# Draining attention's output by head halves, with new order strings for the five engines

## The chip, the cores and the metric

One NeuronCore of a Trainium2 chip runs the whole program. The metric is the device time of one execution in microseconds (us); the kernel before is given by three executions and their median.

## The reference, cut to what matters

The inputs are q, k, v of shape (4 batches, 8 heads, 768 tokens, 64), eight memory keys and values per head, and the weights of two layers of width 512.

```python
for c in range(24):                                  # chunks of 32 queries
    k_ctx = k[:, :, l_start:r_end]                   # 16 keys to the left, 8 to the right
    scores = scale * q_c @ concat([mem_k, k_ctx]).T  # 64 keys a query
    a = softmax(scores)
    out[:, :, c_start:c_end] = a @ concat([mem_v, v_ctx])
x = out, heads side by side                          # (4, 768, 512)
gate = sigmoid(sum_k conv_w[k] * x shifted by k)     # causal convolution, 5 taps
x = (gate * (x @ w_val)) @ w_out
xn = (x - mean) / sqrt(var + 1e-6) * g_ln
out = x + relu(xn @ w_ch1) @ w_ch2                   # 512 -> 2048 -> 512
```

## The kernel before, in words

The 3072 tokens are 24 sub-blocks of 128 tokens (n = 0 to 23). A block (j = 0 to 12) is one sub-block at both ends and two in between. Each sub-block goes through attention (`attend`, or `attention32` in float32 for the first ones), each block then through mixing (`mix_steps`: convolution, gate, two projections, layer norm) and the feed-forward part (`ffn`: `ch1` and then `second`, or from j = 3 on `products` and `fast_finish`, a scheme of seven products instead of eight). Matmuls are split: a float32 value is held as two float16 parts, and three of the four part products are summed.

**What attention leaves.** The last matmuls of a sub-block (L541, in float32 L445) write two PSUM tiles `pv[0]` and `pv[1]`, one for each group g of 64 tokens; partitions 0 to 63 hold one head of a pair (e = 0) and 64 to 127 the other (e = 1). `activations` copies them with a scale into `xT` in four instructions of 64 partitions x 256 values. ScalarE (ACT) does all four at L395 for n under 2 (`EVAC_ACT`) and n of 8 and up (`NEVAC`); for n = 2 to 7 VectorE (DVE) does those with e = 1 at L397. All of them done, ACT and DVE make the float16 parts `x` (L547, L548).

**PSUM banks.** `bank` hands out banks in rotation. From j = 3 on (`fast[0]`) only the two buffers of the tag "ps" rotate, so `pv[0]` and `pv[1]` take both, and whoever calls `bank` next gets the buffer of `pv[0]`, the one after it that of `pv[1]`. For n = 9, 11, ... 21 the next two in program order are the scores of the next sub-block (`s_ps`, L349) and a second projection of mixing (`yps`, L619).

**What sets the order.** Every instruction gets a one-letter label while the program is made (`mark`): a and b attention of even and odd sub-blocks, x and y mixing of even and odd blocks, f the first layer of the feed-forward part with its evacuation, g its second layer and end, t sums of weights, m, p, q the conversion of the mixing weights, of w_ch1 and of w_ch2, l and w loads, s the start. `pin` then reads one string for each engine (`ORDER`): "b48f24a48" means the next 48 instructions with label b, then 24 with f, then 48 with a; "a+2" takes the one that stands two places further on among those left of its label. Each instruction gets a dependency on the one before it in the string, so the string is the engine's order. An engine works in that order; one that waits holds up all behind it.

**Names of the steps below.** In the start: convolution taps L583, gate tanh L587, gate product L603, projection `yps` L619 with its copy L624, layer norm L626 to L646, transposed result `xnT` L651, weight conversion L230 and L231. Later: `ch1` matmuls `c_ps` L804, their copy `ft` L717, operand parts `hb`/`w` L721 to L728, `products` matmuls `acc` L769, transposing DMAs of the probabilities `pT` (L521) and of the normed rows `xn` (L666).

Of the kernel before, what the change touches and what calls it, by code (L numbers as in the profile page):

```python
# [49 lines left out]
PLAN = "w1 a4 l1 a1 w3 m2 w1 m1 a1 x1 w1 1_1 m1 l1 x1 w1 x1 w1 x2 w1 x3 a2 w1 x1 1_1 a1 m1 a2 w1 a1 x1 1_1 a3 1_2 x1 1_3 2_1 x2 1_1 l1 x4 f2 w1 1_1 m1 x1 w2 1_1 2_1 m1 1_1 2_2 x1 2_1 x1 1_1 2_1 f1 a1 w1 m1 a1 2_2 f1 x1 f2 2_1 w1 a2 1_1 2_1 l1 f1 a4 m1 w1 x1 f1 2_3 w1 a2 1_2 x1 1_1 2_4 f1 a1 x1 f2 x1 f2 a2 f1 x1 a2 x1 a1 f2 x1 a1 x3 a1 f1 a1 x1 a1 f1 a1 x1 f1 a1 x1 f1 a1 f3 a1 f1 a2"  # L50
ORDER = {
    "PE": (
        "s24a+16a+16a+16a+16a+16a+16a+16a+16a+16a+16a+16s8a69a+4a+4a+4a+4a+4a+4a+4a+4a+20a+20a+20a+20a+20a+20a+20a+20a+20a+20a+20"
        "a+20a+20a+20a+20a+20a20m16m+16x6m8x8b16x2m8x4b4a16b16x4mp24f3f+13f+13f+13a4p8f3a16p16f2y3p8f14q8f6p8y8fy2q8y3py3q16y2q8"
        "y3b17f5q8f11gf14g3q8gf2gq8gb4gqag3a16b16g5ff+23a4f23a10ba6g12f71g2g+1g+1gx10b48x14f12x12f12g6f14x12f10x6gag12x18b48f12g6"
        "f24a48f12g54a48bf48y24f12g12f12b48g6f36g6f24y24g12af48b48y24a48g12f12g30a48g12bg6x36f60x12f36b48f12g10f24g8f12g24ag12f12"
        "b48f24a48x24f12g84a48g18bg12f96b48y24g10f12g8f36y24ag54b48g12f12a48y24f36g18bg36a48g30b48x12f48x12f24x12f24g10x12f48g20a"
        "f12b48g24a48f12x24f24g30bg42a48g42f12b48f36y24f24g18f24y24f48g12ag12f12b48f24a48y24f12g72bg30a48g24b48f36x12f12x12f36x12"
        "f12x12g30f24g12f24b48af24g18f12a48x24g12f12g12bg30a48g54f96b48y36g10y12f48g20ag24f24b48g18a48y24f24g12bg84a48f60b48f36"
        "x36f12g42f12x12f24ag18b48f36a48x24f12g66bg18a48g24f72g18f12g12f12b48g12f24y48f24g30b48f12y24f36g24x12g42x24g30x12f96g30"  # L60
        "f24g12f12g12x6g6f36x6f24g78f36g30f156g96"),
    "DVE": (
        "s2a7s2a2m2bm+2m+2mxx+3xx+2xx+1x3x+3xx+2xmx2bxabx2pbmbm+2bm2bpxmxbx3ax6ax3paxa3papm3pb+3ma2pyy+3yy+2yy+1qypy2y+3ypyy+1y2p"
        "yqpqympyp3q2mpmqy2pybb+2ybpyqba+3x+20ybypy3by3pybybyqybpqmqpyqbq2pq2aa+2a3qyaqaba2qbaqbgfb3qbx+22a2b2xtxtbtxfx2txbax+2ft"
        "xx+1x2t+2fx2bxbqtb+6xbxy+20bt2xb2txtxtbtxbtat+1a2qftat2xafx2axa2xbxa+8xbx3axax5a3xa2txty+22fabtt+2xtft3gt2ga2t2t+1yab3t"
        "b2y2fby4b2fy2t3bftby+3ytyty+1yfybyt2t+1t3b2ybt2t+1fbya3bfa2t2yt2yb2t2a2yaa+7a2y2a4y2t+2x+20ty2ay3fy6tyt3fbyx+22tayxtxbx"
        "b2xtb2g2b2xt+1xtx3x+3xx+2f5bfb+7bxbf3x2f2bxb3fbxx+1a3faf2xafa3a+7fxa2fax2a3x8ax6f3y+20f2xy+22fxb4y2bg4g+1x+20g2by+2byy+1"
        "b2faf4b+8fy3bfyf4ybyfy2b2y3b2a2bayby+1ya2fafaf2yfaa+8a2fa2y2a3by8ay6fbx+22bf4yb6fyag4b+7b2xg+1g2b2xx+2xf4x+1x2fbfx2bx+3x"
        "f2y+20bf2xx+1fx3fxx+1a2fa2xa4a+7axf2af2axa2fx5ax5ax5b3y+22b3xf5b2xfbb+7g4g+1yg2yay+2yy+1ybyf2bf2y2y+3b2fybfyy+1y2byf3bf2"
        "yfy+1a2x+20yafa2fa2faya+7f2a3fa2y2ay2ay12bfyf2x+22bfb2fb3yfb2b+8gbg2agx2g+1g2x+2xx+1x2bf5x6fb3x2bxby+20f3xfbf2x+1x2a3f5"  # L70
        "a5a+8a2bfa4x2ax2ax12b2fxf4b3xfb2g3y+22gg+1g2y2y+2abf2b+7f3yy+1b2fby4f2y+3f2x+20y2fy+1y3fb4a3ya2y+1yf5a3a+7x+22ya2fy2a4"
        "y14af3yf2b2fyb6g4g+1g2xbb+7f3xfb2afx+2xy+20fb2x+1xbx3x+3f4bx2x+1xfbx2fxx+1a5xfa3f2a+7xa2f2a4xfx7ax8f3xbf2b2xb3fbg3y+22g"
        "g+1g2y2y+2yy+1yf3yf3x+20b2b+8b2y2y+3ybabyy+1b2y2byfbyf5y+1yfyf4bxfyx2x+1x2x+2xy2x+1y14f3x2x+1xf2xyfxg2xg2g+1g2xf4x2f8xf4"
        "x2fx10fx3f6gf2g2fgg+1gfg5"),
    "Activation": (
        "s3a2msm2a4x4mbpaxbpxpb2ap3b2pa2b+1y2qypybmm+1q2yfq2mpyqpmyfpq2pba+1pab+3yp2f2pqb+3yqabqbq2b2fqa2bx2bx2qfbt+1af2b+2btfax2"
        "a2xbqt+1taxafaxb2a+2axfbfabxt+1tb2at+1a2yty3bfb2b+2f2bft+1ta2yfayt+1btfyab2a2fya+2bt+1ya2b3tfya5yt+1xtb2x3bb+2f+1f4af2b"
        "a2fxbf+1f2x2a3a+2b4faxbf+1xfab2fx2bfx2a4y2gy2b2abf+1fb+2f2af4bf+1a2ybyf2aya2a+2b5faybyab2f+1f2y2b3yfaya4xgb+2bax3f+1f6ab"
        "afxf+1f2xa3a+2b2xb3afx2b3af+1f2x4b2fbb+2a4gy2ay2f+1f2a2baf4byfyf+1f2aya2a+2b4faybyaf+1fbfby2by2b2fba3b+2a2gx2f+1f2a3x2b"
        "f4bxfxf+1xf2a3b2a+2fb6ax2af+1f2x3a2xfb3a2gyay2b+2f+1fyf2bf3a2fyaf+1bf2ya3ya+2b4fb3yabyaf+1f2y3fyb2gbb+2a4xf+1f2a2xbafx2"  # L80
        "f2afbfxf+1fxfa3a+2xb6axfaxbf+1fbfx4fb2abb+2ga3y3f+1f6ayb2y2ff+1f2yb5x2fxyxyf+1fyfy3fgf+1x2f7f+1f2x2ff+1x2f3gf4"),
    "Pool": (
        "as4s+2s2ab2ta+1ab2gbaba+1ab2aba+1ba2b3a"),
    "SP": (
        "s+1s3w2l2w2l3w2lw2lw2lqwlw3q2l2waqlyaa+1yay2b+2ga2b+2b+2b2a+2a+2a+2x2axaxg2b+2b+2b3a+2a+2a+2a2y4g2b+2b+2b+2b2a+2a+2a+2a2"
        "x4b+2b+2b+2g2b2a+2a+2a+2a2y4b+2b+2b+2bgba+2ga+2a+2a2x4b+2b+2b+2b2a+2a+2g2a+2a2y4g2b+2b+2b+2b2a+2a+2a+2a2x4b+2gb+2gb+2b2"
        "a+2a+2a+2ay2ay2g2b+2b+2b+2b2a2x4gb2gy4g2x2g4"),
}
PASSES = ((0, 0), (0, 1), (1, 0))

# [19 lines left out]
def chunk_attention_moe_kernel(ctx: ExitStack, tc: tile.TileContext,  # L110
# [276 lines left out]

    def activations(n, xT, pv, c_pv):
        c0 = KW - 1
        for g, t in enumerate(pv):  # L390
            for e in range(2):
                pp = slice(e * 64, (e + 1) * 64)
                o = xT[pp, :, c0 + g * 64:c0 + (g + 1) * 64].rearrange("p a (c q) -> p a c q", q=CHUNK)
                if e == 0 or n < EVAC_ACT or n >= NEVAC:
                    nc.scalar.activation(out=o, in_=t[pp, :, :, e, :], func=AF.Copy, scale=c_pv if isinstance(c_pv, float) else c_pv[pp])  # L395
                else:
                    nc.vector.tensor_scalar(out=o, in0=t[pp, :, :, e, :], scalar1=c_pv if isinstance(c_pv, float) else c_pv[pp], scalar2=None,  # L397
                                            op0=ALU.mult)


    def attention32(n, d, u):
# [46 lines left out]
        if n == 0:  # L448
            fill(FILLS[3])
        activations(n, xT, pv, 1.0)  # L450
        if not d["f32"]:
            xs = xT[:, :, KW - 1:KW - 1 + SUB]
# [13 lines left out]
    def attend(n, d, u):  # L466
# [625 lines left out]
```

## Time and profile before

| what | us |
|---|---|
| three executions, median (lowest to highest) | 725.04 (724.04 to 728.56) |
| the profiled execution, its time | 727.59 |
| the profiled execution, span from its first to its last instruction | 725.5 |
| TensorE matmuls busy (share of the span) | 705.8 (97%) |
| VectorE, ScalarE, GpSimd busy | 621.6, 462.1, 15.5 |

The times of rows are those of the profiled execution, counted from its first instruction. PE is TensorE's matmuls, PEld its weight loads, DVE VectorE, ACT ScalarE, POOL GpSimd, SP the engine that issues most DMAs. L395 is line 395 of the kernel before. A granted clock of 1.00 is 2.4 GHz and one of 0.50 is 1.2 GHz. Matmuls overlap in the records, so the mean duration of one is longer than the distance from one to the next.

### The profile page before, as it was taken

The numbers are of one execution on the slowest core, as the hardware profiler recorded it, in microseconds if no ns is written. First come the engines' busy times: TensorE is split into PE (matmuls) and PEld (weight loads), VectorE is DVE, ScalarE is ACT, GpSimd is POOL, SyncE is SP. The second block draws the span as 40 slices with busy tenths as digits, with TensorE's granted clock in tenths as the row PEclk, the third lists the DMA queues.
The fourth block names the chain that finished last, engine by engine and source line by source line (L and its number), as shares of the span: only waits on it lengthen the run. The fifth ranks groups of instructions, "written<-read, shape, count | busy, mean of one in ns | idle before, by whom it ended". The sixth has DMA issues, their size and how long they took to land.

```text
span 725.5 us, 18122 instructions
## 1 busy us (share of the span) xinstructions
PE 705.8 (97%) x7629; PEld 570.4 (79%) x7629; DVE 621.6 (86%) x1339; ACT 462.1 (64%) x734; POOL 15.5 (2%) x37
## 2 busy tenths in 40 slices
PE   8899999999999999999999999999999999999998
PEld 7687768657758888878778878878878878878897
DVE  4889999999999979989979989879988987885443
ACT  4578775656665885884776786775787685562330
POOL 2010010000000000000000000000000000000000
PEclk9999999999999999999999999999999999999999
DMA  9997323241242323232322233133033012101001
GB/s 348 414 410 289 93 44 109 55 119 42 44 96 81 98 58 95 55 63 74 111 38 74 49 100 102 18 93 111 16 93 112 17 30 31 31 19 42 2 15 44
DMA packets 64448, 67.76 MB, mean 93 GB/s; under 512 B 47856, under 2 KB 48112, under 8 KB 64368
## 3 DMA queue, kind: packets, MB, share of 16 engines
q1 hardware_dynamic: 64080, 66.59, 30.8%
q8 instruction: 59, 0.97, 0.6%
q14 instruction: 21, 0.17, 0.1%
q10 hardware_dynamic: 288, 0.02, 0.0%
HBM read 49.30 MB, written 6.29 MB: 77 GB/s over the span
## 4 chain that ended last, share of the span: by engine, by line
PE 43%; DVE 32%; ACT 9%; DMA 4%; issue 3%; DVEq 0%; ACTq 0%
PE c_ps L804 18%; PE acc L769 12%; DVE gt L583 5%; PE val L601 4%; PE yps L619 4%; PE acc L849 3%; DMA xn<-xh 3%; DVE w L293 2%; ACT xT L395 2%; ACT bd L499 1%; PE s_ps L349 1%; DVE vs L526 1%; DVE bd L500 1%; DVE bs L626 1%; DVE ks L503 1%
## 5 line engine op out<-in xcount | busy, mean ns | idle before, releaser
L804 PE MATMUL c_ps<-xn,w 128*128 128x256 f16 (+1 forms) x2304 | 255.3, 268 | 3.1 <-DMA xn<-xh 2.5
L804 PEld LDWEIGHTS <-w 128*128 128x128 f16 x2304 | 216.0, 98 | 32.8 <-DMA xn<-xh 3.4
L583 DVE SCALAR_TENSOR_TENSOR gt<-xT,cw_sb,gt 128x256 f32<-128x256 f32 (+1 forms) x208 | 87.5, 457 | 0.9
L769 PEld LDWEIGHTS <-hb 128*128 128x128 f16 x756 | 73.0, 98 | 11.5
L769 PEld LDWEIGHTS <-w 128*128 128x128 f16 x756 | 72.8, 98 | 11.8 <-ACT w L727 2.3
L717 ACT ACTIVATE ft<-c_ps 128x512 f32<-128x512 f32 x72 | 40.8, 592 | 48.3 <-DVE y L787 16.5
L849 PE MATMUL acc<-w,hb 128*128 128x512 f16 (+2 forms) x280 | 64.3, 374 | 0.7 <-DVE hb L818 0.7
L769 PE MATMUL acc<-w,hb 128*128 128x256 f16 (+1 forms) x360 | 64.6, 278 | 0.0
L601 PE MATMUL val<-x,wv 128*128 128x256 f16 (+1 forms) x528 | 60.0, 268 | 0.9 <-DVE x L548 0.9
L769 PE MATMUL acc<-w 128*128 128x256 f16 x342 | 58.8, 273 | 0.0
L619 PE MATMUL yps<-wo,hg 128*128 128x512 f16 x252 | 56.7, 379 | 0.1
L601 PEld LDWEIGHTS <-wv 128*128 128x128 f16 x528 | 49.6, 98 | 7.2 <-issue 1.1
L769 PE MATMUL acc<-spare,hb 128*128 128x256 f16 (+1 forms) x324 | 54.9, 276 | 0.0
L769 PE MATMUL acc<-spare,w 128*128 128x256 f16 x324 | 53.7, 273 | 0.0
L619 PEld LDWEIGHTS <-hg 128*128 128x128 f16 x252 | 24.0, 98 | 27.7 <-DVE hg L607 0.6
L849 PEld LDWEIGHTS <-hb 128*128 128x128 f16 x264 | 25.2, 98 | 19.7 <-DVE hb L818 1.5
L727 ACT ACTIVATE hb<-ft 128x1024 f16<-128x1024 f32 x18 | 18.9, 1052 | 26.7 <-DVE ft L726 26.6
L395 ACT ACTIVATE xT<-pv,c_pv 64x256 f32<-64x256 f32 x70 | 32.4, 465 | 4.9 <-PE pv L541 4.0
L727 ACT ACTIVATE w<-ft 128x1024 f16<-128x1024 f32 x18 | 19.0, 1054 | 22.5 <-DVE ft L726 22.4
L362 ACT ACTIVATE sc<-sc,c_exp 128x512 f32<-128x512 f32 x19 | 13.7, 719 | 29.3 <-DVE sc L361 22.3
L500 DVE SCALAR_TENSOR_TENSOR bd<-qt,s,bd 64x512 f16<-64x512 f32 x38 | 28.3, 745 | 3.1 <-ACT bd L499 2.3
L499 ACT ACTIVATE bd<-qt,s 64x512 f16<-64x512 f32 x38 | 27.1, 713 | 1.9 <-DVE s L200 1.5
(188 smaller groups left out, 1209.8 us busy)
## 6 DMA issues: line engine op xcount, KB each, us to landing
vt<-in_v_dram SPq DMA_DIRECT2D x24, 512.0 KB, 4.9
kt<-in_k_dram SPq DMA_DIRECT2D x24, 384.0 KB, 3.8
qt<-in_q_dram SPq DMA_DIRECT2D x24, 256.0 KB, 2.8
out_dram<-y SPq DMA_DIRECT2D x23, 256.0 KB, 2.3
w<-in_w_ch_dram SPq DMA_DIRECT2D x5, 1023.5 KB, 9.3
spare<-in_w_ch_dram SPq DMA_DIRECT2D x4, 1023.8 KB, 13.0
w<-in_w_ch_dram SPq DMA_DIRECT2D x4, 1023.8 KB, 14.1
spare<-in_w_ch_dram SPq DMA_DIRECT2D x3, 1023.5 KB, 7.7
```

The costliest lines, as they stand in the source:

```text
L293: nc.vector.scalar_tensor_tensor(out=lo, in0=w, scalar=s, in1=hi, op0=ALU.mult, op1=ALU.subtract)
L395: nc.scalar.activation(out=o, in_=t[pp, :, :, e, :], func=AF.Copy, scale=c_pv if isinstance(c_pv, float) else c_pv[pp])
L499: nc.scalar.activation(out=hi, in_=src, func=AF.Copy, scale=s[pp, 0:1])
L500: nc.vector.scalar_tensor_tensor(out=lo, in0=src, scalar=s[pp, 0:1], in1=hi, op0=ALU.mult, op1=ALU.subtract)
L583: nc.vector.scalar_tensor_tensor(out=o, in0=xT[:, hp, 0:n, kk:kk + SUB], scalar=cw_sb[:, kk, hp:hp + 1], in1=o, op0=ALU.mult, op1=ALU.add)
L601: nc.tensor.matmul(out=t[:, u, 0:T], lhsT=l, rhs=r, start=(x == 0), stop=(x == len(todo) - 1))
L619: nc.tensor.matmul(out=t, lhsT=l, rhs=r, start=(x == 0), stop=(x == len(todo) - 1))
L717: nc.scalar.activation(out=ft[:, at:at + 2, :].rearrange("p x (m n) -> p m x n", m=2), in_=t.rearrange("p (m x n) -> p m x n", m=2, x=2), ...
L727: nc.scalar.activation(out=o[0][1], in_=ft, func=AF.Copy)
L769: nc.tensor.matmul(out=o, lhsT=l, rhs=r, start=first, stop=(p == half // 2 - 1 and u2 == 1 and end[t] == x))
L804: nc.tensor.matmul(out=t[:, u * T:(u + 1) * T], lhsT=l, rhs=r, start=(x == 0), stop=(x == len(todo) - 1))
L849: nc.tensor.matmul(out=a[:, 0:n], lhsT=l, rhs=r, start=(first and x == 0), stop=(end and x == len(todo) - 1))
```

## The change

The loops of `activations` change places: first both groups' halves with e = 0, then both groups' halves with e = 1. The strings of all five engines are replaced; each holds the same number of every label as before, in another order. Nothing else changes. The core of the diff, with TensorE's strings whole and the first line of VectorE's and ScalarE's:

```diff
     "PE": (
-        "s24a+16a+16a+16a+16a+16a+16a+16a+16a+16a+16a+16s8a69a+4a+4a+4a+4a+4a+4a+4a+4a+20a+20a+20a+20a+20a+20a+20a+20a+20a+20a+20"
-        "a+20a+20a+20a+20a+20a20m16m+16x6m8x8b16x2m8x4b4a16b16x4mp24f3f+13f+13f+13a4p8f3a16p16f2y3p8f14q8f6p8y8fy2q8y3py3q16y2q8"
-        "y3b17f5q8f11gf14g3q8gf2gq8gb4gqag3a16b16g5ff+23a4f23a10ba6g12f71g2g+1g+1gx10b48x14f12x12f12g6f14x12f10x6gag12x18b48f12g6"
-        "f24a48f12g54a48bf48y24f12g12f12b48g6f36g6f24y24g12af48b48y24a48g12f12g30a48g12bg6x36f60x12f36b48f12g10f24g8f12g24ag12f12"
-        "b48f24a48x24f12g84a48g18bg12f96b48y24g10f12g8f36y24ag54b48g12f12a48y24f36g18bg36a48g30b48x12f48x12f24x12f24g10x12f48g20a"
-        "f12b48g24a48f12x24f24g30bg42a48g42f12b48f36y24f24g18f24y24f48g12ag12f12b48f24a48y24f12g72bg30a48g24b48f36x12f12x12f36x12"
-        "f12x12g30f24g12f24b48af24g18f12a48x24g12f12g12bg30a48g54f96b48y36g10y12f48g20ag24f24b48g18a48y24f24g12bg84a48f60b48f36"
-        "x36f12g42f12x12f24ag18b48f36a48x24f12g66bg18a48g24f72g18f12g12f12b48g12f24y48f24g30b48f12y24f36g24x12g42x24g30x12f96g30"
-        "f24g12f12g12x6g6f36x6f24g78f36g30f156g96"),
+        "s32a+16a+16a+16a+16a+16a+16a+16a+16a+16a+16a+16a69a+4a+4a+4a+4a+4a+4a+4a+4a+20a+20a+20a+20a+20a+20a+20a+20a+20a+20a+20"
+        "a+20a+20a+20a+20a+20a20m16m+16m8x14b16x6m8a12p8a4b14p8mb6x4p8f3f+13f+13f+13a4p8f3a16p24f22p8y16pq8yq8ygyfy5q8b17f5q16f11"
+        "q8f6gq8g2f2q8f6g2b4qaf2a16b16g10ff+23a4f23a10ba6g12f47g2b48f36g+1g+1x48f26g8x6af10g6f12x18f24b48g12a48g4f12g44a48bg6f48"
+        "y24g12f12b48f12g12f36y12f12y12f12g6f12g6af24b48y24a48g12f24g24a48g24bx24f84x24f12b48f48g30af36b48f12g12a48x24g84a48g12b"
+        "g30f84b48f12y24g30f36y12f12ag24y12g6f12b48g24a48y24f36bg54a48g30b48x24f48x12f48x12g18f48g24ag30b48f24a48x24f24g30a48g42b"
+        "g24f60b48f24y12f12y36f48g30af12g12f12b48g12f12a48y24f12g48bg66a48f72g10b48f24g20x24f12x12f36x12ag12f12b48g12f12a48x24f24"
+        "g60ba48g54f96b48g10y12g8y12f12g12f36y24ag24f12b48f24a48y24g6f12g42bg12a48g54f84b48g10f12x24f36x12f12g20x12ag24f12g6b48"
+        "f12g12a48x24f24g72a48g24bf96b48g42f48g12y48f24b48g6f12y24f12g78x48g30f84g18f12g12f48x6g12x6g12f36g6f12g108f84g12f84g36"
+        "f24g48"),
     "DVE": (
-        "s2a7s2a2m2bm+2m+2mxx+3xx+2xx+1x3x+3xx+2xmx2bxabx2pbmbm+2bm2bpxmxbx3ax6ax3paxa3papm3pb+3ma2pyy+3yy+2yy+1qypy2y+3ypyy+1y2p"
+        "sa5sa2s2a2m2bm+2m+2mxx+3xx+2xx+1x3x+3xx+2x4mxbxbpbmab2m+2xbxpxaxm2xbx3ax3mxaxaxapxap2am3p2a2b+3yy+3yy+2yy+1ypmyqyy+3ypy"
...
     "Activation": (
-        "s3a2msm2a4x4mbpaxbpxpb2ap3b2pa2b+1y2qypybmm+1q2yfq2mpyqpmyfpq2pba+1pab+3yp2f2pqb+3yqabqbq2b2fqa2bx2bx2qfbt+1af2b+2btfax2"
+        "s4a2m3a4x4mbpxbaxp3ab3p2bpa2y2pqfb+1y2mq2m+1qyqpmbpyq2ypa+1fbqpmpfypapqb+3b+3b2fqaypq3b2fqbab2axqfxfxt+1xa2b+2abftx2faqx"
...
     def activations(n, xT, pv, c_pv):
         c0 = KW - 1
-        for g, t in enumerate(pv):
-            for e in range(2):
+        for e in range(2):
+            for g, t in enumerate(pv):
                 pp = slice(e * 64, (e + 1) * 64)
                 o = xT[pp, :, c0 + g * 64:c0 + (g + 1) * 64].rearrange("p a (c q) -> p a c q", q=CHUNK)
                 if e == 0 or n < EVAC_ACT or n >= NEVAC:
```

## Rows read from the trace of the kernel before

**Rows 1.** The page: engines' busy time, and TensorE's costliest group

```profile
PE 705.8 (97%) x7629; PEld 570.4 (79%) x7629; DVE 621.6 (86%) x1339; ACT 462.1 (64%) x734; POOL 15.5 (2%) x37
...
L804 PE MATMUL c_ps<-xn,w 128*128 128x256 f16 (+1 forms) x2304 | 255.3, 268 | 3.1 <-DMA xn<-xh 2.5
```

**Rows 2.** Busy time by stage: stretch, PE, PEld, DVE, ACT, POOL, clock, DMA

```profile
0.00:50.00 50.00, 42.48 (x494) 37.15 (x494) 36.16 (x88) 27.25 (x39) 7.30 (x15) 0.93 0.98 389
50.00:225.00 175.00, 172.81 (x1590) 121.12 (x1589) 171.60 (x364) 118.13 (x183) 3.38 (x10) 1.00 0.37 109
225.00:700.00 475.00, 468.60 (x5274) 391.80 (x5273) 405.52 (x874) 313.96 (x508) 4.82 (x14) 1.00 0.24 60
700.00:725.50 25.50, 21.96 (x278) 20.36 (x275) 8.31 (x15) 2.77 (x5) 0.00 (x0) 1.00 0.09 32
```

**Rows 3.** TensorE's waits, 225 to 700 us: us in total, times, longest

```profile
PE c_ps L804 <- DMA xn<-xh: 2.3, 3, 0.9
PE acc L769 <- ACT w L727: 1.7, 2, 1.0
PE val L601 <- DVE x L548: 0.9, 1, 0.9
PE c_ps L804 <- ACT ft L717: 0.6, 1, 0.6
PE s_ps L349 <- ACT xT L395: 0.3, 1, 0.3
PE acc L769 <- DVE w L728: 0.2, 1, 0.2
```

**Rows 4.** Timeline of the start: start, duration, instruction, idle before it

```profile
18.76 3.49 DVE L583 SCALAR_TENSOR_TENSOR gt<-xT,cw_sb,gt 128x128 f32<-128x128 f32 x13
...
22.18 1.22 DVE L231 SCALAR_TENSOR_TENSOR wo<-w,spare 128x1024 int32<-128x1024 int32 x1
...
24.81 0.63 ACT L587 ACTIVATE gt<-gt 128x512 f32<-128x512 f32 x1 [0.28 <-DVE gt L583]
...
25.87 0.74 DVE L603 SCALAR_TENSOR_TENSOR gt<-gt,val 128x256 f32<-128x256 f32 x2
...
26.43 5.37 PE L619 MATMUL yps<-wo,gt 128*128 128x512 f32 x8 [2.30 <-DVE gt L603]
...
32.46 0.69 DVE L626 BATCH_NORM_STATS2 bs<-y 128x6 f32<-128x512 f32 x1 [1.75 <-ACT y L624]
...
36.98 0.55 DVE L646 TENSOR_SCALAR xh<-y,mv,rt 128x512 f32<-128x512 f32 x1
...
37.67 2.05 PE L651 MATMUL xnT<-eye,xh 128*128 128x128 f32 x8 [1.61 <-DVE xh L646]
```

**Rows 5.** Stretches of the start at a lower clock, columns as in rows 2

```profile
26.40:32.50 6.10, 6.07 (x16) 3.07 (x16) 4.35 (x12) 2.24 (x4) 0.00 (x0) 0.72 1.00 414
...
37.60:42.50 4.90, 4.83 (x42) 4.79 (x43) 4.33 (x7) 2.45 (x2) 0.00 (x0) 0.68 1.00 396
```

**Rows 6.** Timeline of one handover of banks, after sub-block 19

```profile
524.50 0.85 PE L541 MATMUL pv<-pT,vs 64*128 64x64 f16 x46 [0.17 <-DMA pT<-p]
...
525.35 1.15 ACT L525 ACTIVATE vs<-vt,s 128x1024 f16<-128x1024 f32 x1 [1.57 <-PE pv L541]
...
526.41 1.91 ACT L395 ACTIVATE xT<-pv,c_pv 64x256 f32<-64x256 f32 x4
...
527.39 0.95 PE L349 MATMUL s_ps<-ks,bd 128*64 128x64 f16 x48
...
528.37 1.89 PE L619 MATMUL yps<-wo,hg 128*128 128x512 f16 x8
```

**Rows 7.** Timeline of two of the waits of rows 3

```profile
379.23 0.28 PE L769 MATMUL acc<-wo,w 128*128 128x256 f16 x1 [0.77 <-ACT w L727]
...
389.40 1.80 PE L601 MATMUL val<-x,wv 128*128 128x256 f16 x15 [0.90 <-DVE x L548]
```

More of the change, by code (lines that the diff above doesn't have):

```diff
@@ L61 @@
-        "f24g12f12g12x6g6f36x6f24g78f36g30f156g96"),
-    "DVE": (
-        "s2a7s2a2m2bm+2m+2mxx+3xx+2xx+1x3x+3xx+2xmx2bxabx2pbmbm+2bm2bpxmxbx3ax6ax3paxa3papm3pb+3ma2pyy+3yy+2yy+1qypy2y+3ypyy+1y2p"
[L64 to L74, printed above, removed]
@@ L75 @@
-    "Activation": (
-        "s3a2msm2a4x4mbpaxbpxpb2ap3b2pa2b+1y2qypybmm+1q2yfq2mpyqpmyfpq2pba+1pab+3yp2f2pqb+3yqabqbq2b2fqa2bx2bx2qfbt+1af2b+2btfax2"
[L77 to L81, printed above, removed]
+        "s32a+16a+16a+16a+16a+16a+16a+16a+16a+16a+16a+16a69a+4a+4a+4a+4a+4a+4a+4a+4a+20a+20a+20a+20a+20a+20a+20a+20a+20a+20a+20"
@@ new lines @@
+        "g24f60b48f24y12f12y36f48g30af12g12f12b48g12f12a48y24f12g48bg66a48f72g10b48f24g20x24f12x12f36x12ag12f12b48g12f12a48x24f24"
+        "g60ba48g54f96b48g10y12g8y12f12g12f36y24ag24f12b48f24a48y24g6f12g42bg12a48g54f84b48g10f12x24f36x12f12g20x12ag24f12g6b48"
+        "f12g12a48x24f24g72a48g24bf96b48g42f48g12y48f24b48g6f12y24f12g78x48g30f84g18f12g12f48x6g12x6g12f36g6f12g108f84g12f84g36"
+        "f24g48"),
+    "DVE": (
+        "sa5sa2s2a2m2bm+2m+2mxx+3xx+2xx+1x3x+3xx+2x4mxbxbpbmab2m+2xbxpxaxm2xbx3ax3mxaxaxapxap2am3p2a2b+3yy+3yy+2yy+1ypmyqyy+3ypy"
+        "y+1qy3pqpypmpyp2q2pm2ypyqyqybb+2yb3y2py2byqby3pa+3y3pybqbqpqabq2ma+2a3q2ybpqax+20x+22ayaqpaqbgaqbfb3qb4a2ty+20xtxbxtfx2t"
+        "xfx+2xx+1bax2bx2tt+2xtxfxqb+6xtxbfbxtbtabta2ta2bxa3btxtfqx2t+1xtxtxy+22xb2x3a+8xax2ax3ataxaba2ftxatxtt+2tft3ba2b2tbytagy"
+        "tytt+1by2tgyfb3t2ytybfytbtftx+20y+3ybyy+1bt2t+1fyby2t3fbtybty2ba2t+1t2ataya2b2a2ta+7tfayay3ayta2yayt+2y2ayty6tyf2t3ybt2y"
+        "tx+22ax6b4t+1xgx2x+3gtb2xx+2x2f2bf3bxfb+7b2xf5b4fbxa3f2x+1a2f2axa2a+7fxa6fx15axy+20y+22f4xbfxfby2b3g4g+1bg2b3f5y+2yay+1"
+        "y2fb+8bybx+20yf5yb3fb2y4a2yayfbf2yy+1fa5y2a+8a2fba3fyay4ay5ay2by4bfbf3bfbyb3fyag4g+1g2b+7b2x+22xb2xx+2xx+1f2xy+20f3xb2f"
+        "x2x+3x2f5x+1bx2fx2x+1a3xa2f3xa2faa+7fa2faxba2xax2ax12f2xf4xb7y+22g4g+1g2bb+7afy2b2y+2fybf2b2fy+1y2fybyy+3yx+20f3yf2y+1y3"
+        "fyby+1a2fa3f3yax+22ayfaa+7a2fa4by13ay3fyf2b3f2b3yfb2g4g+1g2x2x+2b+8fxf4ax+1b2fxb5fx2f2bxfx4fx3fxx+1a3fa2xa2faa+8faxaf2a3"
+        "xaxafx2ax6y+20x7f4y+22b4fb2xfb2g4g+1g2bb+7f5y2y+2x+20afyy+1y4y+3b2fybyb3fy+1f3y3fbyy+1a3f2ayafa3fa+7ya2bax+22afayafy3a"
+        "y12b3ybf5ybfb2g4g+1g2bb+7xf2af3xx+2xy+20bx+1bfx3bfxfx+3bfbfbfx2x+1xfx2bxx+1a3fa2f2a2x2faa+7fa2fabaxa2x6ax9y+22f3xf3xbgb2"
+        "g3g+1g2b4ybf2ab+8f2yfy+2yy+1fby3bfyfy+3y2y+1b3yb2f2yf2ybyy+1yf3yfx+20f2by2xy2x2x+1xy2fy6xy4f2yf2x+2yxfg4g+1g2x+1x2x+1x4"
+        "f6x2f2x2f6xfx4f3xf3xf2x8fg4g+1fgfg2f2g3"),
@@ new lines @@
+    "Activation": (
+        "s4a2m3a4x4mbpxbaxp3ab3p2bpa2y2pqfb+1y2mq2m+1qyqpmbpyq2ypa+1fbqpmpfypapqb+3b+3b2fqaypq3b2fqbab2axqfxfxt+1xa2b+2abftx2faqx"
+        "a2fat+1bx2tb2a+2b2axf2abxt+1bta2yay2t+1tfb3f2b+2ybt+1tfa3fyby2t+1ta2f2b2aa+2bt+1y2a2bftyba4yxt+1abtx3b3b+2f+1f6bxa2fab"
+        "f+1f2a2xaxa+2b5fa2x2f+1f2b2x2bx2fa4y3gb2abb+2f+1f3af3bayaff+1bf2aya2y2a+2b7afy2baf+1f2yb2yfby2a5xga2xb+2bf+1f2afxbxf4f+1"
+        "x2f2xa3a+2b5fax2ab2f+1f2x3afxb3gbb+2a4f+1fyfy2bfyf3a3bfyf+1f2y2a3a+2b4fab3y2f+1f2aby3byfb2ga2b+2a2x2f+1xf2a2fabfxf2abfx"
+        "f+1f2xa3a+2b5xb2axfbxaf+1f2x4afba3bgby4b+2af+1f6ba3bfyf+1f2y2a3a+2b7ayfyabf+1f2y2b2y2fa3bga2x2b+2f+1f3bx2f3a2bfaf+1fxfa3"
+        "x2b2a+2b3faf+1x2af2x3fxb3agbab2a2f+1yf2b+2ay2f4yb2ff+1f2y3b4fx2bf+1y2xf2xy4fgf+1f4xf2x2ff+1f2xff+1f3x2gf4"),
@@ L82 @@
     "Pool": (
-        "as4s+2s2ab2ta+1ab2gbaba+1ab2aba+1ba2b3a"),
+        "s4s+2s2a2b2a+1batbab2ga+1ab3aa+1abab2ab"),
     "SP": (
-        "s+1s3w2l2w2l3w2lw2lw2lqwlw3q2l2waqlyaa+1yay2b+2ga2b+2b+2b2a+2a+2a+2x2axaxg2b+2b+2b3a+2a+2a+2a2y4g2b+2b+2b+2b2a+2a+2a+2a2"
-        "x4b+2b+2b+2g2b2a+2a+2a+2a2y4b+2b+2b+2bgba+2ga+2a+2a2x4b+2b+2b+2b2a+2a+2g2a+2a2y4g2b+2b+2b+2b2a+2a+2a+2a2x4b+2gb+2gb+2b2"
-        "a+2a+2a+2ay2ay2g2b+2b+2b+2b2a2x4gb2gy4g2x2g4"),
+        "s+1s3w2l2w2lwl2w4lw2lqw3l2q2wlal2qyaa+1a2y3b+2gab+2a+2b+2b2x2a+2a+2a2x2b+2b+2b2g2ba+2a+2a+2a2y4b+2b+2b+2b2a+2a+2ga+2ga2"
@@ L88 @@
+        "x4b+2b+2b+2b2g2a+2a+2a+2a2y4b+2b+2b+2bgba+2ga+2a+2a2x4g2b+2b+2b+2b2a+2a+2a+2a2y4b+2b+2b+2b2g2a+2a+2a+2a2x4b+2b+2b+2bg2b"
+        "a+2a+2a+2a2y4b+2gb+2b+2b2ga2x4g2b2y4g2x2g4"),
 }
```

## The prediction

> **What bounds the kernel now.** I read the page's first part, then busy time by stage, then who TensorE waits for, then the timeline at those places. The page shows PE busy for 705.8 of 725.5 us [rows 1]. By stage, PE is idle for 50 - 42.48 = 7.5 us in the first 50 us, for 175 - 172.81 = 2.2 from 50 to 225, for 475 - 468.60 = 6.4 from 225 to 700 and for 25.5 - 21.96 = 3.5 at the end, where the last result is scaled and sent [rows 2]. So TensorE sets the end everywhere after the start, with VectorE close beside it from 50 to 225 (171.60 of 175), and a reordering of the same instructions can only change 19.6 us of idle time and what a lower clock costs. The clock was not at its upper level in two stretches of the start: the mean grant was 0.72 over 6.1 us and 0.68 over 4.9 us, each behind a wait [rows 5]. Had the upper level held, they would have been 6.1 x 0.28 + 4.9 x 0.32 = 3.3 us shorter at most.
>
> The sum is made against the profiled execution: 727.59 us, that is its span of 725.5 and 2.1 around it. It lies 2.55 above the median of the runs shown, 725.04; I carry the difference over to the median.
>
> **The edit of the loops.** It adds and removes no instruction. For n = 2 to 7 it doesn't do what it says: ACT has the e = 0 halves and DVE the e = 1 halves, each in group order before and after, so no engine's order changes. For the other 18 sub-blocks ACT's four copies run 0/0, 1/0, 0/1, 1/1 (group/half) in place of 0/0, 0/1, 1/0, 1/1. The bank of `pv[0]` is then free after the third copy, not the second; that of `pv[1]` after the fourth, as before. Four copies took 1.91 us, 0.48 each [rows 6], so the first bank is handed over 0.48 us later.
>
> This matters where the next user of the bank comes at once: after sub-blocks 9, 11, ... 21, seven places, of which rows 6 show one. There `pv` ended at 525.35, the copies began at 526.41 (ACT first did the 1.15 us of L525), the second was done at 526.41 + 0.96 = 527.37 and `s_ps` began at 527.39: it took the bank the moment it was free. The fourth was done at 528.32 and `yps` began at 528.37 [rows 6]. In the new string TensorE has exactly 24 matmuls of 256 columns between `pv` and `s_ps` at each of the seven places ("b48f24a48", "b48g12f12a48" and the like; before it was 18 to 54). One takes 255.3 / 2304 = 0.111 us [rows 1], so they last 2.66. The third copy is done (start of the copies after `pv`'s end) + 1.43 later. With the 1.06 of rows 6 that is 2.49: no wait. The copies began 1.39, 1.07, 2.03, 1.07, 3.11, 1.06 and 2.86 us behind `pv` at the seven places; with the same lateness the new order waits 0.2 + 0 + 0.8 + 0 + 1.9 + 0 + 1.6 = 4.5 us. That is the upper end; the lower is nothing, if ACT's new string starts them in time. It moves what delayed the copies: a `hb` of 1.04 us that stood among them at the fifth place goes behind, and so does the 1.15 us of L525, into their middle, at the seventh. I take 0.6, near the lower end, as at the place shown.
>
> Here a rule of the Trainium skill speaks against the edit. What the rows show: the bank of `pv[0]` was written again 0.02 us after its second copy ended [rows 6]. "Perfetto Trace Analysis", section Optimizing Tensor Performance, says that independent matmul groups should rotate through different PSUM banks so that the copying of one overlaps the matmuls of the next. Draining both banks side by side holds both longer, so by the rule the edit loses up to the 4.5 us above; by the place shown it loses nothing. It is the slower rival below.
>
> **The strings in the start.** Before, the chain that ends PE's 2.30 us wait is: taps L583 (13 from 18.76, three more behind a conversion and a maximum), tanh L587 at 24.81, gate product L603 at 25.87, `yps` at 26.43 [rows 4]. The new DVE string runs all 16 taps together ("x4mxbxb" in place of "xmx2bxabx2"): 13 took 22.18 - 18.76 = 3.42, so 16 take 4.21 and end at 22.97; the conversion of 1.22 comes next, the tanh of 0.63 runs beside it, and the first product starts at about 24.2, 1.7 us sooner. PE's second eight gram matmuls (0.6 us) move behind `yps`, so its wait shrinks from 2.3 to about 1.2. What is late next is the layer norm: from L626 at 32.46 to the end of L646 at 37.53 it took 5.07 us, for which PE waited 1.61 [rows 4]. The new string puts a conversion (1.22), two softmax passes of 0.7 and some small ones inside that chain, about 2.8 more, and moves 16 gram matmuls (1.4 us of PE) ahead of `xnT`. Net: 1.7 sooner, 2.8 later, 1.4 of work done meanwhile, some 0.3 gained; with a shorter first wait a part of the 3.3 us of lower clock may come back. Bounds: from 1.5 lost (the 2.8 in full against 1.3 of cover) to 0.3 + 3.3 = 3.6 gained. I take 1.0 gained, near the lower gain, since a second wait stays.
>
> **The strings from 50 us on.** From 225 to 700 TensorE waited nine times for over 0.15 us by the groups shown, 6.0 us in all, mean 0.67 [rows 3]. Where the new string puts the waiting matmul later or its producer sooner, a wait goes. The `acc` at 379.23 waited 0.77 for L727 [rows 7]; L727 now stands ahead of two copies of 0.7, which covers it. The `val` at 389.40 waited 0.90 for L548 [rows 7]; `val` now comes 36 matmuls later, 3.9 us. Read so place by place, the waits for `val`, for L727 (one whole, the other by half), for `s_ps` after L395, for L728 and one of three for the transposed `xn` go: 0.9 + 1.3 + 0.3 + 0.2 + 0.7 = 3.4.
>
> What comes in their place can't be read from the rows of before. The strings also bring matmuls forward past work that their producers still have ahead, by 1 to 6 us in some 20 places; many of these producers only waited, and come forward too. From below it costs nothing; from above each of 20 places costs the mean wait, 13.4. DVE (86% busy) and ACT (64%) [rows 1] have room to follow, so I take a fifth: four waits of 0.67, 2.7 us. In the last stage nothing changes: TensorE's last 24 matmuls, their scaling and the output transfer stay.
>
> **Sum.** -1.0 (start) - 3.4 (waits gone) + 0.6 (banks) + 2.7 (new waits) = -1.1. The profiled execution would go from 727.6 to 726.5, the median from 725.04 to 723.9.
>
> **Rivals.**
> *A clear gain.* The new strings take away nearly all they can: four fifths of 6.4 + 2.2, 6.9 us, and 3.0 in the start with the clock: 725.0 - 9.9 = 715.1. For it: all seven handovers now have the same cover, and the start's first wait is shortened. Against it: the same producers at the same durations, and DVE already busy for 98% of the stretch from 50 to 225 [rows 2].
> *Slower: the banks come late.* Place: `s_ps` behind `pv`, seven times. Price: the 4.5 us above; and where a late `s_ps` makes the softmax and its transposing DMA late, the next `pv`, which waited for such a DMA for 0.17 us at 524.50 already [rows 6], pays it once more, 9.0 in all. It decides once the copies begin over 1.2 us behind `pv`'s end. 725.0 + 4.5 = 729.5, or 734.0 carried on. Against it: only 0.3 us of waits for L395 were seen [rows 3]. The rule of the Trainium skill quoted above is the reason to take it seriously.
> *Nothing.* The strings' gains and new waits cancel: 725.0, between 723 and 727.
>
> **Chances.** Forecast 0.55, its own range 720.5 to 728; clear gain 0.15; banks late 0.18, half of it carried on; nothing 0.12. A measurement of this kernel can tell about 1%, 7.25 us. Faster than 717.8 are most of the clear gain and a sliver of the forecast, 0.14; slower than 732.3 is the carried half of the bank case, with a sliver of the forecast, 0.11; the rest, 0.75, is the same within 1%. Range: 716.5 to 732, which cuts off about a tenth on either side.
>
> **What would show it.** Right: PE busy for 704 to 707 us; in the waits of TensorE from 225 to 700 us no `val` for L548 and no `acc` for L727 of 0.7 or more, and 4 to 7 us of idle time there; `yps` of the start at 24 to 25.5 us with a wait near 1.2. The bank case shows as `s_ps` (L349) waiting for L395 for over 2 us in total; the clear gain as less than 2 us of idle time from 225 to 700. I am wrong if the idle time outside these places moves the sum: new waits of `acc` or `c_ps` for ACT beyond 6 us in total, or VectorE idle from 50 to 225 where before it was not.

## The result and the profile after

The changed kernel took 717.6 us in the median (716.99 to 718.77), beside 726.8 for the kernel before in the same comparison: ratio 0.9877, 95% interval 0.9833 to 0.9921. Run once more against other runs of before it took 719.2 (717.17 to 719.96) beside 726.3: 0.9896, 0.9871 to 0.992. So it is faster by 1.0 to 1.2%, 7 to 9 us. The forecast was 1.1 us; the time lies 1.1 us inside the low end of the range (716.5) and near the rival that was called a clear gain (715.1).

The page of the changed kernel, the lines that answer to [rows 1]:

```profile
span 716.6 us, 18133 instructions
PE 703.5 (98%) x7629; PEld 570.5 (80%) x7629; DVE 617.9 (86%) x1339; ACT 460.6 (64%) x734; POOL 16.8 (2%) x37
...
L804 PE MATMUL c_ps<-xn,w 128*128 128x256 f16 (+1 forms) x2304 | 254.8, 268 | 1.2 <-DMA xn<-xh 0.8
```

The span went from 725.5 to 716.6, by 8.9: PE's idle time fell from 19.7 to 13.1 (6.6 less) and its busy time from 705.8 to 703.5 (2.3 less) for the same 7629 matmuls. That is about what the clock makes: the mean grant of the profiled execution was 0.995 before and is 0.998 here. Busy time by stage, columns as in [rows 2]:

```profile
0.00:50.00 50.00, 44.05 (x524) 39.43 (x525) 38.34 (x94) 28.86 (x41) 6.75 (x14) 0.97 0.98 391
50.00:225.00 175.00, 173.38 (x1593) 122.21 (x1592) 171.13 (x369) 118.60 (x185) 4.38 (x9) 1.00 0.34 104
225.00:700.00 475.00, 472.92 (x5366) 396.96 (x5364) 404.22 (x873) 311.91 (x507) 5.64 (x14) 1.00 0.24 62
700.00:716.60 16.60, 13.14 (x156) 11.93 (x153) 4.20 (x7) 1.19 (x2) 0.00 (x0) 1.00 0.14 49
```

Beside [rows 2], PE's idle time is 5.95 (before 7.52) in the first 50 us, 1.62 (2.19) up to 225, 2.08 (6.40) up to 700 and 3.46 (3.54) at the end. The middle gave 4.3, two thirds of the idle time that went. Its waits, answering to [rows 3]:

```profile
PE c_ps L804 <- DMA xn<-xh: 0.8, 1, 0.8
PE acc L769 <- DVE w L728: 0.6, 1, 0.6
PE tot L211 <- ACT ks L484: 0.3, 1, 0.3
PE c_ps L804 <- ACT ft L717: 0.2, 1, 0.2
```

`val` for L548, `acc` for L727 and `s_ps` for L395 are gone. Four waits, 1.9 us, stand where there were nine of 6.0. Only the 0.8 for `xn` is at a matmul that waited before (603.55 then, 594.90 now); the other three are at new places.

The timeline of the start, answering to [rows 4], then the clock of one stretch, columns as in [rows 5]:

```profile
17.87 0.16 PE L283 MATMUL gram<-wv_col,ones 128*128 128x1 bf16 x1 [0.77 <-DVE wv_col L280]
18.87 4.54 DVE L583 SCALAR_TENSOR_TENSOR gt<-xT,cw_sb,gt 128x128 f32<-128x128 f32 x16
...
19.01 0.63 PE L272 MATMUL gram<-wo 128*128 128x128 bf16 x8 [0.97 <-DVE wo L231]
...
19.48 4.97 PE L601 MATMUL val<-xT,wv 128*128 128x128 f32 x28
...
24.46 0.41 DVE L603 SCALAR_TENSOR_TENSOR gt<-gt,val 128x256 f32<-128x256 f32 x1
...
26.01 3.60 PE L619 MATMUL yps<-wo,gt 128*128 128x512 f32 x8
...
30.31 0.68 DVE L626 BATCH_NORM_STATS2 bs<-y 128x6 f32<-128x512 f32 x1
...
36.91 0.54 DVE L646 TENSOR_SCALAR xh<-y,mv,rt 128x512 f32<-128x512 f32 x1
...
37.60 1.13 PE L651 MATMUL xnT<-eye,xh 128*128 128x128 f32 x8 [0.52 <-DVE rs L375]
```

```profile
20.00:24.00 4.00, 4.00 (x24) 4.00 (x23) 3.93 (x14) 3.24 (x4) 0.00 (x0) 0.57 1.02 413
26.40:32.50 6.10, 5.87 (x59) 3.65 (x58) 5.82 (x13) 4.01 (x5) 0.00 (x0) 1.00 1.02 426
37.60:42.50 4.90, 4.73 (x46) 4.38 (x47) 4.79 (x6) 3.12 (x4) 0.00 (x0) 1.00 1.02 417
```

All 16 taps are one run; `yps` starts behind other work of PE, not behind a wait; it took 3.60 us where it took 5.37. The clock fell once, to 0.57 in the mean over 20 to 24 us, behind the waits of 0.77 and 0.97, and not at the two places of [rows 5].

### The profile page after: what moved, and what is told of

Same layout as the page of the kernel before. It is cut to its first block, busy times and chain, and to the rows that moved or that the text cites. A ratio compares the mean times of both kernels' runs of the same rounds, so it can differ in the third digit from the quotient of the medians.

```text
span 716.6 us, 18133 instructions
## 1 busy us (share of the span) xinstructions
PE 703.5 (98%) x7629; PEld 570.5 (80%) x7629; DVE 617.9 (86%) x1339; ACT 460.6 (64%) x734; POOL 16.8 (2%) x37
## 4 chain that ended last, share of the span: by engine, by line
PE 58%; DVE 26%; ACT 6%; DMA 5%; issue 4%; SPq 0%; POOL 0%; DVEq 0%; ACTq 0%
PE c_ps L804 24%; PE acc L769 13%; PE val L601 6%; PE yps L619 5%; PE acc L849 5%; DMA xn<-xh 4%; DVE gt L583 3%; PE s_ps L349 2%; DVE w L293 2%; DVE w L231 2%; PE pv L541 1%; DVE bs L626 1%; ACT ft L717 1%; DVE sc L361 1%; DVE mx L360 1%
## 5 line engine op out<-in xcount | busy, mean ns | idle before, releaser
L717 ACT ACTIVATE ft<-c_ps 128x512 f32<-128x512 f32 x72 | 40.8, 594 | 34.4 <-PE c_ps L804 7.8
L727 ACT ACTIVATE hb<-ft 128x1024 f16<-128x1024 f32 x18 | 19.0, 1055 | 29.2 <-DVE ft L726 29.0
L395 ACT ACTIVATE xT<-pv,c_pv 64x256 f32<-64x256 f32 x70 | 29.3, 461 | 9.1 <-PE pv L541 8.8
L727 ACT ACTIVATE w<-ft 128x1024 f16<-128x1024 f32 x18 | 18.9, 1052 | 15.7 <-DVE ft L726 12.7
L816 ACT ACTIVATE hb<-c_ps 128x512 f16<-128x512 f32 (+1 forms) x22 | 12.8, 589 | 22.3 <-PE c_ps L804 22.1
```

The source lines that it names most:

```text
L717: nc.scalar.activation(out=ft[:, at:at + 2, :].rearrange("p x (m n) -> p m x n", m=2), in_=t.rearrange("p (m x n) -> p m x n", m=2, x=2), ...
L727: nc.scalar.activation(out=o[0][1], in_=ft, func=AF.Copy)
```

## The experiments

Theory 1: the new strings make the gain, in the start and in the middle separately, and the edit of the loops gives nothing. Rivals: the loops make it (1); the banks come late and the gain is net of that (2); the early start pushes the later waits away (3); later ones on the loops (4), the clock (5) and hand-made moves (6) are in the expectations. A kernel whose strings I composed has them on fewer lines, so its line numbers are 2 lower (L395 is L393).

Runs of one kernel differ by up to 6 us, and their mean granted clock by up to 0.008. One least-squares fit through the 165 runs that have a clock on record, with a base for each kernel and one common slope, gives 0.57 us for each 0.001 of clock (twice the standard error: 0.06) and 0.7 us of scatter round it. The last column is that base, the time at a clock of 1.000, with twice its standard error; where the question is smaller than the clock's part, I compare by it. ("Fills" are warming matmuls and "moves" are edits of the strings by hand; both are told below.)

| kernel | median us | ratio to before, 95% | clocks | at 1.000 |
|---|---|---|---|---|
| before | 726.3 | 1 | 0.992 to 1.000 | 724.2 ± 0.3 |
| the change | 717.6 | 0.9833 to 0.9921 | 0.997 to 0.999 | 716.6 ± 0.7 |
| the change again | 719.2 | 0.9871 to 0.992 | 0.993 to 0.999 | 717.0 ± 0.6 |
| loops only | 727.8 | 1.0003 to 1.004 | 0.993 to 0.998 | 725.0 ± 0.5 |
| strings only | 719.9 | 0.9891 to 0.9948 | 0.993 to 0.997 | 716.6 ± 0.7 |
| start new | 723.6 | 0.9945 to 0.9985 | 0.993 to 1.000 | 722.2 ± 0.5 |
| start old | 720.4 | 0.9903 to 0.9958 | 0.992 to 0.998 | 718.9 ± 0.6 |
| before, three moves | 724.7 | 0.9957 to 0.999 | 0.995 to 1.000 | 723.1 ± 0.5 |
| before, five moves | 725.3 | 0.9972 to 1.0005 | 0.992 to 0.998 | 722.8 ± 0.5 |
| before, fills | 722.6 | 0.9929 to 0.9968 | 0.999 to 1.000 | 722.3 ± 0.5 |
| before, fills, new loops | 725.0 | 0.9966 to 0.9999 | 0.993 to 1.000 | 724.5 ± 0.4 |
| the change, fills | 716.1 | 0.9828 to 0.9885 | 1.000 | 716.2 ± 0.7 |
| the change, fills, old loops | 716.2 | 0.9834 to 0.9878 | 0.999 to 1.000 | 716.1 ± 0.7 |

**Loops only, and strings only.** The two halves of the change:

```diff
-        for g, t in enumerate(pv):
-            for e in range(2):
+        for e in range(2):
+            for g, t in enumerate(pv):
```

with the old `ORDER`; and the new `ORDER` with the old loops.

> The changed loop order of the copies out of PSUM, with the old five strings. Theory 1 (the gain is in the strings): within 1.5 us of the kernel before, no wait of s_ps for L395 over 0.5 us, and the old waits of 225 to 700 us (val for L548, acc for L727) still there, about 6 us of PE idle in that stretch. Rival 1 (the loop order itself makes the gain): 3 to 9 us faster. Rival 2 (banks come late): 3 to 9 us slower, with s_ps waiting for L395 at the handovers.

> The new five strings with the old loop order. Theory 1: 7 to 10 us faster than the kernel before, as the whole change is, with 2 to 3 us of PE idle between 225 and 700 us. Rival 1: at most 5 us faster. Rival 2: 1 to 4 us faster than the whole change, so 10 to 13 us faster than before.

At equal clock the loops alone cost 0.9 ± 0.6 us and the strings alone gain 7.6, as much as the whole. Rival 1 falls. Of rival 2 the mechanism is there, under the old strings, where theory 1 expected no such wait over 0.5. TensorE's waits from 225 to 700 us with the loops only:

```profile
PE s_ps L349 <- ACT xT L395: 2.0, 4, 1.2
PE c_ps L804 <- DMA xn<-xh: 0.8, 2, 0.4
PE acc L769 <- ACT w L727: 0.7, 1, 0.7
PE val L601 <- DVE x L548: 0.6, 1, 0.6
```

`s_ps` waits 2.0 for L395 where it waited 0.3 [rows 3], four times. The longest, of the same kernel:

```profile
355.90 0.81 ACT L395 ACTIVATE xT<-pv,c_pv 64x256 f32<-64x256 f32 x2
...
357.25 0.83 ACT L395 ACTIVATE xT<-pv,c_pv 64x256 f32<-64x256 f32 x2
357.77 0.95 PE L349 MATMUL s_ps<-ks,bd 128*64 128x64 f16 x48 [1.19 <-ACT xT L395]
```

ACT does two copies, something else, then two more; with the new order the first bank needs the third, done at 357.7, and `s_ps` starts there. In sum these waits added nothing there, though: others shrank by more, and PE's idle time from 225 to 700 us is 4.7 (6.4 before). It grew in the start, from 7.5 to 8.8 in the first 50 us, where one `pT_ps` waited 1.04 for L395. In the changed kernel the same handover has all four copies in a row and no wait:

```profile
354.45 1.66 ACT L395 ACTIVATE xT<-pv,c_pv 64x256 f32<-64x256 f32 x4
...
355.88 1.10 PE L349 MATMUL s_ps<-ks,bd 128*64 128x64 f16 x48
```

**Start and rest.** The instructions that the kernel before starts in its first 60 us in one order, all others in the other (start new: old loops; start old: new loops). In words:

```diff
-"PE": old for all
+"PE": new for those begun before 60 us, old for the rest   (all five strings alike)
```

> New order for the instructions that the kernel before starts in its first 60 us, old order for all later ones, old loops. Theory 1 (a start worth 2.4 us and a middle worth 6, each by itself): 1.5 to 3.5 us faster than before, val's and acc's waits in 225 to 700 us as before, about 6 us idle there. Rival 3 (an earlier start pushes all later waits away): 6 to 9 us faster, 2 to 3 us idle there.

> Old order for the instructions that the kernel before starts in its first 60 us, new order for all later ones, new loops. Theory 1: 5 to 7.5 us faster than before, two stretches at a lower clock in the start as before, about 2 us of PE idle in 225 to 700 us. Rival 3: at most 3 us faster, with the later waits back.

At equal clock the start gives 2.0 and the rest 5.3; their sum, 7.3, is the whole within the noise (7.4: 724.2 - 716.8, the mean of its two rows). Rival 3 falls: with the new start alone `acc` still waited 1.9 us for L727 and `val` 0.6 for L548, and PE's idle time from 225 to 700 us was 6.0. With the old start the profile has one stretch at a lower clock, not the two expected.

**The clock.** The changed kernel once more, and with 58 warming matmuls of the start's kind (`idle`, 128x128) put where TensorE waits in the start; the kernel before likewise with 83:

```diff
-FILLS = (32, 64, 8, 16)
+FILLS = (32, 64, 8, 74)
-"...a20m16m+16m8x14b16x6m8a12p8a4b14p8mb6x4p8..."
+"...a20m16a13m+16a17m8x14b16x6m8a12+28p8a4+28b4a20b10p8mb6a8x4p8..."
```

> The whole change once more, for its clock. In the runs so far a run's time follows its own mean granted clock (one line through 63 runs of six kernels: 0.60 us for each 0.001, 0.7 us of scatter round it), and at clock 1.000 that line has the whole change at 716.5, new strings with old loops at 716.4, the kernel before at 724.0. Theory 1 (the loop order gives nothing; the two differ by the clock of the start): 716.5 plus 0.6 for each 0.001 below 1.000, in whatever mix of clocks. Rival 4 (the loop order is worth 2 us with the new strings): runs of the same clock 1.5 to 2.5 us below new strings with old loops.

> The whole change, and 58 more warming matmuls (128x128, 0.05 us each) on TensorE in four places of the start where it waits: 13 before the first column sum, 17 before gram of wo, 20 before the second block's pv, 8 before xnT. Theory 1 (a wait of TensorE near 18 and near 37 us is what lowers the granted clock there): clock 1.000 in every run, 716 to 717 us, a spread of at most 1.5 us. Rival 5 (the clock falls for another reason, or the fills delay the work behind them): clocks from 0.993 to 0.999 as before, 717 to 721 us.

> The kernel before, with 83 more warming matmuls in its start: 13 before the first column sum, 42 before the first yps, 28 before xnT. Theory 1: clock 1.000 in every run, 723.5 to 724.5 us, so 2 us faster in the median. Rival 5: clocks and times as the kernel before, 724 to 729 us.

Rival 5 falls. With fills the change ran at a granted clock of 1.000 each time, within 715.82 to 716.61; without them within 716.99 to 719.96. The start of the run with fills:

```profile
17.00:26.00 9.00, 8.05 (x100) 6.92 (x98) 8.68 (x24) 6.39 (x13) 0.00 (x0) 1.00 1.03 414
26.00:32.50 6.50, 6.27 (x68) 4.30 (x67) 6.37 (x14) 4.23 (x5) 0.00 (x0) 1.00 1.02 423
32.50:42.50 10.00, 9.83 (x122) 8.87 (x119) 9.68 (x30) 6.39 (x9) 0.22 (x2) 1.00 1.01 413
```

TensorE's waits at the four places fell to 0.2 and less; a wait of 0.7 before `yps` came in exchange. For the kernel before they gave 3.7 us in the median, more than was expected; 1.9 of these are more than its own line gives (722.3 against 724.2). Its profile has 4.2 us of idle time from 225 to 700, not 6.4: with the start 3 us earlier the waits there fell otherwise. So an earlier start can move later waits, which is rival 3's mechanism, though the new start alone did not do it. Why is open.

The change with fills is also the fastest version, 1.4% below before; beside the change alone its gain is the clock (716.2 against 716.8 at 1.000).

**The loops at one clock.** The same pair of fills with the loop order turned round:

> The old strings with the 83 warming matmuls and the new loop order, to price the loop order at one clock: beside the same with the old loops (722.3). Theory 1 (under the old strings the third copy frees the bank later, 0.9 us by the line through the runs): 722.7 to 723.7, waits of s_ps for L395 1 to 2 us in all. Rival 2: 3 us or more slower. Rival 1: faster than 722.

> The new strings with the 58 warming matmuls and the old loop order, beside the same with the new loops (716.1). Theory 1: 715.6 to 716.6, clock 1.000, so that the loop order is worth nothing there. Rival 4 (the loop order is worth 2 us under the new strings): 717.5 to 718.5.

Under the old strings the loops cost 724.5 - 722.3 = 2.2 us, more than expected: `s_ps` waited 2.3 for L393 in the middle (0.6 with the old loops) and one `pT_ps` in the start 2.3. Under the new strings they cost nothing (716.2 against 716.1, each ± 0.7), so rival 4 falls. TensorE's waits of the first of the two, whole span:

```profile
PE s_ps L347 <- ACT xT L393: 2.3, 4, 1.5
PE pT_ps L429 <- ACT xT L393: 2.3, 1, 2.3
```

The traces put the cost at the wait in the start. Its timeline:

```profile
34.29 0.65 ACT L393 ACTIVATE xT<-pv 64x256 f32<-64x256 f32 x2 [2.40 <-PE pv L443]
...
41.63 0.65 ACT L393 ACTIVATE xT<-pv 64x256 f32<-64x256 f32 x2
...
42.07 1.16 PE L429 MATMUL pT_ps<-eye,sc 128*128 128x128 f32 x8 [2.27 <-ACT xT L393]
```

Again two copies, then much else, then two. With the old loops this `pT_ps` started at 39.86 without a wait, 2.2 us sooner, and `pv` of a later sub-block was 2.2 sooner as well (245.48 against 247.69). From 225 to 700 us PE's idle time is 3.9 with the new loops and 4.2 with the old, so the waits of `s_ps` there added nothing in sum. This kernel's clock was not held by its fills (0.993 to 1.000), so its price goes by the fit after all.

**Moves by hand.** The kernel before, with the producers of three of its waits put earlier, and nothing else:

```diff
 ACT, for 379.23:  -...x2b3af+1f2x4b2fbb+2a4g...   +...x2b3af+1f2x4fb3b+2a4g...
 ACT, for 489.80:  -...x2af+1f2x3a2xfb3a2g...      +...x2af+1f2x3a2fxb3a2g...
 DVE, for 389.40:  -...g4g+1yg2yay+2yy+1...        +...g4g+1ygagyy+2yy+1...
```

> The kernel before, with three instructions moved earlier in its strings: two of L727 on ACT (for the waits at 379.23 and 489.80) and one of L548 on DVE (for 389.40); together 2.6 us of waits. Theory 1 (a wait that goes in this stretch stays gone, nearly whole): 2 to 2.8 us faster at equal clock, idle in 225 to 700 us near 4. Rival 6, the step of the prediction (the slack is used up and new waits take most of it back): 0 to 1 us faster, idle 5 to 6.4.

The three waits went, and 1.0 us at equal clock came of 2.6, which is rival 6's side. One new wait alone took 1.4. The timeline behind it:

```profile
378.28 1.53 DVE L498 SCALAR_TENSOR_TENSOR bd<-qt,s,bd 64x512 f16<-64x512 f32 x2 [2.48 <-ACT bd L497]
...
379.84 0.69 DVE L662 TENSOR_TENSOR xh<-xh,xh 128x512 f16<-128x512 f32 x1
...
380.45 1.22 DVE L726 TENSOR_TENSOR w<-ft,w 128x1024 f16<-128x1024 f32 x1
...
381.73 0.28 PE L767 MATMUL acc<-wo,w 128*128 128x256 f16 x1 [1.44 <-DVE w L726]
```

DVE stands 2.48 us for the `bd` that ACT now does later, and the `w` that TensorE needs is queued behind. So its order was changed too:

```diff
 DVE, as well:     -...x5b3y+22b3xf5b2xfbb+7...    +...x5b3y+22b3xf5xfb3b+7...
```

> The three moves again, and two more on DVE (L665 and L729 of the same steps ahead of the two L501), since with three moves DVE stood 2.48 us waiting for the L500 that ACT now ran later, with the L729 that acc needs behind it: the new wait of 1.44 at 381.73. Theory 1 (that new wait is the price of moving one engine's string without the other's): the wait at 381.73 under 0.3, idle in 225 to 700 us 3.5 to 4.2, and 2 to 2.6 us faster than the kernel before at equal clock. Rival 6 (the slack is used up, another wait comes): idle 4.8 or more, at most 1.3 us faster at equal clock.

That wait went as theory 1 says, and another came, 0.99 at 406.00 (`tot`, for L715 on ACT). Idle in the stretch: 6.4, then 5.0, then 4.3. The gain at equal clock is 1.4 ± 0.6, between the two expectations. By idle time about half of what was taken away came back at another place in each round (2.6 taken and 1.4 less; 1.4 taken and 0.7 less); by time at equal clock it was more than half.

## Why the prediction was wrong in size

The time fell inside the range, but at its edge, and the sum had -1.1 us for a change of 7.4 at equal clock. What held was the width of the range, made for the rivals, and not the sum; that is in part luck, for the prediction gave only 0.14 to a time below 717.8. Its signs failed too: 2.1 us of idle time from 225 to 700 where 4 to 7 were foretold, and `yps` at 26.01 where 24 to 25.5 was.

**The failing steps are the third and the fourth term, waits gone at -3.4 and new waits at +2.7.** Together they made -0.7. Followed matmul by matmul through both traces, eight of the nine waits of [rows 3] are gone, but for 0.07 of one, and the ninth went from 0.88 to 0.80: 5.1 of 6.0 went, 1.7 more than forecast. New are three, 0.19 for L717 at 273.46, 0.26 for L484 at 373.92 and 0.58 for L728 at 429.67: 1.0 came, 1.7 less than forecast. Idle time fell by 4.3 there and by 0.6 from 50 to 225. The reason given was right ("many of these producers only waited, and come forward too") and then not used: all five strings move in step, so a matmul that comes forward finds its producer forward too. The `acc` that waited 0.77 for L727 at 379.23 [rows 7], in the changed kernel:

```profile
370.36 1.06 ACT L727 ACTIVATE w<-ft 128x1024 f16<-128x1024 f32 x1
...
373.94 0.27 PE L769 MATMUL acc<-wo,w 128*128 128x256 f16 x1
```

The matmul came 5.3 us forward and its operand, done at 379.17 before and 371.41 here, 7.8. At the waits of 324.95, 389.40 and 489.80 the matmul came 3.7, 2.3 and 7.0 us forward and the operand 4.1, 5.2 and 8.3. That the same holds at the other places where matmuls came forward is argued, not shown, and no run puts one engine's new string beside the old ones. The moves by hand fit it: where one or two engines' orders are changed and the others' are not, about half comes back.

**The waits gone** were named rightly place by place (`val`, L727, L395, L728) and were undercounted: both waits for L727 went whole, the one for L717, which was not named, went too, and two of three for the transposed `xn` (2.3 to 0.8), not one.

**The start, -1.0**, measured 2.0 ± 0.6 at equal clock. The steps held in part: 16 taps took 4.54 (4.21 predicted), the first product started at 24.46 (24.2), and the layer norm from L626 to the end of L646 took 7.14 (7.9; 5.07 before). Wrong was the wait near 1.2 before `yps`: there was none, since PE was at work until 26.01, a part of it at the lower clock (the 28 matmuls of `val` took 4.97 us; before, in two stretches, 1.60 and 2.00). `xnT` came at the same time as before, 37.60, with more work done ahead of it. The lower clock, bounded at 3.3, is a term of its own, and it is no constant of the kernel: it differs from run to run.

**The banks, +0.6**, measured nothing under the new strings (716.2 against 716.1) and 0.9 to 2.2 under the old. The reckoning of the third copy was near: it is done 1.30 us after the copies begin, not 1.43. What differs is that the new strings start the copies sooner and keep them together: at six of the seven handovers all four run in a row from 1.07 to 1.44 us behind `pv` (before, up to 3.11); at the seventh they begin at once, with L525 in their middle. So the third ended 0.05 to 0.30 us before `s_ps` began, at all seven: the cover of 24 matmuls just suffices. The rule cited from the Trainium skill, "Perfetto Trace Analysis", section Optimizing Tensor Performance, was that independent groups of matmuls rotate through different banks, so that the copying of one overlaps the matmuls of the next. Under the old strings the trace agrees with it: with the loops only, the waits for L395 were 2.0 us in the middle and 1.0 in the start. Under the new strings no run shows a loss, since the third copy ends before the next user comes.

**The other terms and rivals.** The end stayed as it was (3.5 both times), and DVE stayed busy from 50 to 225 (171.1). PE's busy time, 703.5, came just below the 704 to 707 foretold. "Nothing" and "slower" fell. "Clear gain" had the right places and was too large in both: 4.9 us of idle time went of its 6.9 behind the start, and 2.0 us came of its 3.0 in it; 7.4 in all at equal clock, where it had 9.9. VectorE's 98% from 50 to 225 was held against it; that stretch had only 2.2 us to give anyway, and the 6.4 lay where VectorE had room.

## What to carry to other kernels

Price a reordering by the idle time of the bounding engine, stage by stage: that is what can go. Here five orders planned anew together took two thirds of it from 225 to 700 us (4.3 of 6.4) and a quarter from 50 to 225 (0.6 of 2.2); of the waits that edits by hand took away, half or less stayed gone. Before comparing kernels within 1%, look at the granted clock of each run, and compare at one clock. A change of access order that costs nothing with one schedule (the loops, 0.0) can cost 1 to 2 us with another, so it is to be tried with the schedule it was made for; and the cost can lie at another place than the one looked at.

## What was not expected of the hardware

The mean granted clock differs between runs of the same kernel on the same chip, 0.992 to 1.000 for the kernel before, and its time follows: 0.57 us for each 0.001, a spread of 722.8 to 729.2. In the profiles a long drop to the lower level (1.2 GHz, a grant of 0.50, against 2.4) shows in the start alone, at up to three places (near 20, 28 and 38 us), each behind waits of TensorE of 0.8 to 2.3 us, and not at each of them in every run. 58 matmuls of 0.05 us that do nothing but fill such waits took the clock of the changed kernel to 0.999 or 1.000 in all ten runs, under either loop order, and the spread from some 3 us to 0.8. The old strings with 83 fills ran at 0.999 to 1.000 with the old loops, but at 0.993 to 1.000 with the new, which left the `pT_ps` wait of 2.27 in the start. That the lower clock stood behind this wait is not shown: the profiled execution ran at 1.000.

The loop order has a gain that no time shows. With the old loops the four copies of a handover began 0.47 to 0.49 us apart (1.91 for the four [rows 6]); with the new, the two for the same 64 partitions began 0.36 to 0.37 apart and only the change of half took 0.47 (1.66 for the four). ScalarE's busy time is 3.1 to 3.9 us lower with the new loops in all four pairs (462.1 and 458.2 under the old strings, 463.7 and 460.6 under the new). Why is not shown. ScalarE was busy for some 64% of the span, and TensorE's time did not follow.
